# Two operands of a chunk made behind the next group's copies, the output product's sums and splits on VectorE, and block 0's reads reordered

## The chip, the cores and the metric

The kernel runs on one core of a Trainium2 chip. The core has five engines that run side by side and meet only at semaphores: TensorE (PE in the profile; its weight loads are PEld), VectorE (DVE), ScalarE (ACT), GpSimd (POOL) and SyncE (SP), which here issues nearly all DMAs. The metric is the device time of one execution in microseconds (us); lower is better. Times are the median of several runs; one further execution was profiled.

## The reference

Three stages on float32 data, one after the other:

```
# 1. attention in chunks of 32 queries, with 16 keys to the left, 8 to the right and 8 memory keys
a = exp(scale * q_c @ k_full.T - max);  out_c = (a / (sum(a) + 1e-9)) @ v_full
# 2. x: (3072, 512)
h = x @ w_in            # (3072, 2048)
x = (h * cos(h)) @ w_out  # (3072, 512)
# 3.
h = max(x @ w1, x @ w2, x @ w3)   # (3072, 768)
y = h @ w_out2                    # (3072, 512)
```

## The kernel before

All matmuls keep float32 accuracy by splitting each operand in a rounded part (hi, made by ACT as a copy to a shorter format) and the rest (lo, made by DVE or POOL as a subtraction of hi from the source); a product is then three passes, hi*hi, hi*lo and lo*hi (PASSES).

**Phase 1** (the first 620 us or so) does stages 1 and 2 in 6 blocks of 512 tokens, each of 16 slots. A slot f does `p1` (x @ w_in for 128 columns of h, 12 matmuls), `chain` (the h*cos(h) of it on ACT and DVE, and the preparing of weights), and `p2` of the slot two before (the product with w_out). Between them lies the attention of the next block, after a table of steps per slot: FIRST for block 0, SECOND and STEADY for the others. In such a table "T1" means: in this slot's chain DVE transposes the attention weights of double chunk 1 (line 286) and SP writes them to DRAM (`ptd`, two buffers, line 287); "l1" or "L1" reads them back in the other layout (`pt`, one buffer, line 292, three DMAs), a small l after the slot's matmuls in SP's order, a capital L at the slot's beginning; "V1" is the product with v (line 305), after which SP loads a later v (line 239). SP and PE take their instructions in the order in which the code is written.

**Phase 2** (from about 620 us) does stage 3 for three pairs of 1024 tokens. Both matmuls of it use a Winograd form of Strassen's scheme: 7 products (PRODUCTS) of half size in place of 8, for which sums and differences of operands are made beforehand and sums of products afterwards. For a pair, `quad(p, q)` does the 7 products of one weight matrix and one slice of d_ff: q = 3*fp + e, chunk fp = 0, 1, 2 and expert e = 0, 1, 2. One product is 6 matmuls. A quad has four PSUM banks, A, E, F and B; A, E and F take two products each: the first is copied out (`snap`: ACT copies a, p5 and p7, line 735) before the second is added on top of it (start=False). So the fifth product of a quad (T2, into bank A) can't start before the copy of a is done, the sixth (B22) not before p5, the seventh (T4) not before p7. The next quad takes the other four banks.

After a quad the results r11, r12, r21, r22 hold the maximum over the experts so far. After e = 2 they make the operands of the output product: `g_oper(n, c)`, n = 0 to 6 for chunk c: a copy on ACT (line 802) and a rest on DVE or POOL (line 803). Operands 0 and 1 are made inside the quad, 2 and 3 at its end (lines 778 and 779) with two differences on POOL (lines 780 and 781), 4 to 6 in the output product. At e = 2 of chunk 2 follows `pair_out(p)`: 7 products of 18 matmuls each (line 836), whose sums are made by ACT (line 821), DVE and POOL (line 824) and stored by SP. While it runs, the operands of the next pair's quads are made from x (`x_ops`; B11, T1, T3, B21, T2, B22, T4; lines 641 and 642), one per product, by ACT and by DVE or POOL.

ACT, DVE, POOL and SP do their instructions in program order; `keep` holds that order as the code is written, `live` counts the buffers of the weight pool (28), and `fetch` loads the weights of a quad three quads ahead.

Of the kernel before, what the change touches and what calls it, by code (L numbers as in the profile page):

```python
# [9 lines left out]
F32 = mybir.dt.float32  # L10
# [36 lines left out]

FIRST = {2: "S0", 3: "S1", 4: "S2", 5: "S3 E01", 6: "E23 N0", 7: "T0 N1", 8: "L0 T1 N2", 9: "V0 l1 T2", 10: "V1 l2 N3", 11: "T3", 12: "V2 l3", 14: "V3"}  # L50
SECOND = {0: "S0", 1: "S1", 2: "E01 S2", 3: "N0 S3", 4: "T0", 5: "E23 N1 L0 S4", 6: "V0 T1", 7: "L1 N2", 8: "S5 T2 N3", 9: "V1 E45", 10: "L2 S6 T3", 11: "V2", 12: "L3 S7", 13: "V3", 14: "E67"}
STEADY = {1: "N0", 2: "T0 N1", 3: "L0", 4: "S4", 5: "V0 T1 N2", 6: "L1", 7: "S5", 8: "V1 T2 N3", 9: "L2 E45", 10: "S6 T3", 11: "V2 l3", 12: "S7", 13: "V3", 14: "E67"}

# [12 lines left out]
NW, NTOP = 28, 2  # L66
# [11 lines left out]
def attn_moe_kernel(ctx, tc, qT, kT, vw, w_in, w_out, w3, w2o, out):  # L78
# [565 lines left out]
    def x_ops(p):  # L644

        u1, u2, v1, v2 = (x2["raw", b, k] for b in range(2) for k in range(2))

        def diff(o, a, b):
            keep(DVE.tensor_tensor(o, a, b, op=ALU.subtract))

        def b11():
            x_get("B11", u1, POOL)

        def t1():
            xs["t1"] = w_tile([128, 2, M], "xt", F32)
            diff(xs["t1"], v1, u1)
            x_get("T1", xs["t1"], DVE)
            live[0] -= 1

        def t3():  # L660
            diff(v1, v2, v1)

        def t2():
            xs["t2"] = w_tile([128, 2, M], "xt", F32)
            diff(xs["t2"], v2, xs["t1"])
            live[0] -= 1
            x_get("T2", xs["t2"], DVE)

        def b22():
            x_get("B22", v2, POOL)  # L670
            live[0] -= 1

        def t4():
            t = w_tile([128, 2, M], "xt", F32)
            diff(t, u2, xs["t2"])
            live[0] -= 1
            x_get("T4", t, DVE)
            live[0] -= 1

        def o3():  # L680
            x_get("T3", v1, POOL)
            live[0] -= 1

        def b21():
            x_get("B21", u2, DVE)
            live[0] -= 1

        def d1():
            xs["t1"] = w_tile([128, 2, M], "xt", F32)
            diff(xs["t1"], v1, u1)  # L690

        def d2():
            xs["t2"] = w_tile([128, 2, M], "xt", F32)
            diff(xs["t2"], v2, xs["t1"])

        def s1():
            x_get("T1", xs["t1"], DVE)
            live[0] -= 2

        def s2():  # L700
            x_get("T2", xs["t2"], DVE)
        return dict(d1=d1, d2=d2, s1=s1, s2=s2, b11=b11, t1=t1, t3=t3, o3=o3, b21=b21, t2=t2, b22=b22, t4=t4)

    def x_free():
        live[0] -= 6
# [14 lines left out]
    def quad(p, q):  # L720

        fp, e = divmod(q, 3)
        bk = dict(zip("AEFB", (t[:, :M] for t in banks(4))))
        seen = set()
        t = {}
        r = post.get(fp)

        def xo(name):
            t[name] = raw_tile(name) if e == 0 else tmp["pool"].tile([128, M], F32, tag="xo", name=name, bufs=6)
            return t[name]  # L730

        def snap(name, b, pool=None):
            o = tr.tile([128, M], F32, tag="r", name=name) if pool else xo(name)
            t[name] = o
            keep(ACT.activation(out=o, in_=bk[b], func=AF.Copy))  # L735

        def add(eng, o, a, b, op=ALU.add):
            keep(eng.tensor_tensor(o, a, b, op=op))  # L738

        for n, (b, i, half, name) in enumerate(PRODUCTS):  # L740
            product(bk[b], wq[p, q, i], half, x2[name], b not in seen, True)
            seen.add(b)
            if n == 0:
                snap("a", "A")
            elif n == 1:
                snap("p5", "E")
            elif n == 2:
                snap("p7", "F")
                add(POOL, t["p5"], t["p5"], t["p7"])
            elif n == 3:  # L750
                add(DVE, t["a"], t["a"], bk["B"])
                if e:
                    add(DVE, r["r11"], r["r11"], t["a"], ALU.max)
                    if e == 2:
                        g_oper(0, fp)
            elif n == 4:
                snap("u2", "A", True)
                add(POOL, t["p5"], t["p5"], t["u2"])
            elif n == 5:
                t["c12"] = raw_tile("c12") if e == 0 else tr.tile([128, M], F32, tag="r", name="c12")  # L760
                add(DVE, t["c12"], t["u2"], bk["E"])
                if e:
                    add(DVE, r["r12"], r["r12"], t["c12"], ALU.max)
                    add(DVE, r["r22"], r["r22"], t["p5"], ALU.max)
                    if e == 2:
                        g_oper(1, fp)
            else:
                add(DVE, t["p7"], t["u2"], bk["F"])
                if e:
                    add(DVE, r["r21"], r["r21"], t["p7"], ALU.max)  # L770
                else:
                    post[fp] = dict(r11=t["a"], r12=t["c12"], r21=t["p7"], r22=t["p5"])
            yield n
        for i in range(4):
            wq.pop((p, q, i))
            live[0] -= 1
        if e == 2:
            g_oper(2, fp)
            g_oper(3, fp)
            add(POOL, r["r11"], r["r22"], r["r11"], ALU.subtract)  # L780
            add(POOL, r["r21"], r["r21"], r["r11"], ALU.subtract)

    def raw_tile(name):
        return tmp["pool"].tile([128, M], F32, tag="raw", name=name, bufs=12)
# [3 lines left out]
    def g_oper(n, c):  # L788

        r = post[c]  # L790
        if n == 1:
            keep(DVE.tensor_tensor(r["r11"], r["r12"], r["r11"], op=ALU.subtract))
        elif n == 2:
            keep(POOL.tensor_tensor(r["r12"], r["r22"], r["r12"], op=ALU.subtract))
        if n in (0, 4):
            g = gp.tile([128, 2, M], F32R, tag="g", name="g")
        elif n in (1, 5):
            g = pre.tile([128, 2, M], F32R, tag="p", name="g")
        else:
            g = w_tile([128, 2, M], "g")  # L800
        src = r[G_SRC[n]]
        keep(ACT.activation(out=g[:, 0, :], in_=src, func=AF.Copy))  # L802
        keep((POOL if G_POOL[n] else DVE).tensor_tensor(g[:, 1, :], src, g[:, 0, :].bitcast(F32), op=ALU.subtract))  # L803
        hB[n, c] = g

    G_POOL = (1, 0, 1, 0, 1, 0, 0)

    def pair_out(p):

# [13 lines left out]
        def add(eng, o, a, b):  # L823
            keep(eng.tensor_tensor(o, a, b, op=ALU.add))  # L824
# [5 lines left out]
        for n, (b, _, _, _) in enumerate(PRODUCTS):  # L830
# [11 lines left out]
            for i in range(2):  # L842
                u = t[i]
                if n == 0:
                    snap(i, "a", "A")
                elif n == 1:
                    snap(i, "p5", "E")
                elif n == 2:
                    snap(i, "p7", "F")
                    add(POOL, u["p5"], u["p5"], u["p7"])  # L850
                elif n == 3:
                    add(DVE, u["a"], u["a"], bk[i]["B"])
                    put(i, 0, 0, u["a"])
                elif n == 4:
                    snap(i, "u2", "A", True)
                    add(POOL, u["p5"], u["p5"], u["u2"])
                    put(i, 1, 1, u["p5"])
                elif n == 5:
                    add(DVE, xo(i, "c12", True), u["u2"], bk[i]["E"])
                    put(i, 0, 1, u["c12"])  # L860
                elif not last:
                    add(DVE, u["p7"], u["u2"], bk[i]["F"])
                    put(i, 1, 0, u["p7"])
                else:
                    for h, eng in enumerate((SP, ACT)):
                        sl = slice(256 * h, 256 * h + 256)
                        add(DVE, u["p7"][:, sl], u["u2"][:, sl], bk[i]["F"][:, sl])
                        c0 = 2 * p * M + 256 * h
                        keep(eng.dma_start(out=out[256 + 128 * i:384 + 128 * i, c0:c0 + 256], in_=u["p7"][:, sl]))
# [183 lines left out]
    got = [AHEAD]  # L1053

    def fetch(upto):
        while got[0] <= upto and got[0] < NP * NG and live[0] + 4 <= NW:
            q_fetch(*divmod(got[0], NG))
            got[0] += 1

# [2 lines left out]
    for p in range(NP):  # L1062
        for q in range(NQ):
            for n in quad(p, q):
                if p == 0 and q == 0 and n < 3:
                    while len(rest) > (2, 1, 0)[n]:
                        p2(*rest.pop(0))
                if n == 0:
                    fetch(p * NG + q + AHEAD)
                if p + 1 < NP:  # L1070
# [3 lines left out]
                    elif (q, n) in DIFFS:  # L1074
                        ops[DIFFS[q, n]]()
        x_free()
        todo = [["b11"], ["s1"], ["o3"], ["b21"], ["s2"], ["b22"], ["t4"]] if p + 1 < NP else []
        for n in pair_out(p):
            if n in (1, 2, 3):
                for c in range(3):  # L1080
                    g_oper(3 + n, c)
# [61 lines left out]
```

## Time and profile before

| | |
|---|---|
| median of 3 runs | 995.16 us (992.09 to 995.8) |
| the profiled execution's own time | 993.47 us |
| its span, first to last instruction | 991.7 us |
| PE busy | 960.4 us (97%) |
| DVE, POOL, ACT busy | 619.5, 477.7, 460.6 us |
| mean granted clock of TensorE | 0.998 of full speed |

PE is busy nearly all the time. So what can be won or lost shows where PE idles, some 31 us of the span in all, and those stretches are found by the view of waits and the timeline of PE. A start in the timeline is when the instruction began on its engine; in brackets stands how long the engine sat idle before it and what released it.

### The profile page before, as it was taken

The page shows a single profiled execution, that of the slowest core. Times are in us where ns is not written, and L with a number is a line of the kernel's source. Part 1 is how long each engine was busy: PE and PEld are TensorE (multiplying, and loading weights), DVE is VectorE, ACT ScalarE, POOL GpSimd, SP SyncE. Part 2 cuts the span into 40 slices and gives each one's busy share as a digit, 9 for nine tenths or more (in the row PEclk, how much of TensorE's full clock was granted, in tenths as well). Part 3 has the DMA queues.
Part 4 walks back from the last instruction along what each step waited for, and adds up shares of the span by engine and source line. Part 5 has one row for each costly group of instructions (what it writes and reads, how often), then busy time and mean ns, then how long its engine had stood idle before and what let it go on. Part 6 is the DMA issues. An engine that isn't in the chain of part 4 may idle for free.

```text
span 991.7 us, 14609 instructions
## 1 busy us (share of the span) xinstructions
PE 960.4 (97%) x5373; PEld 770.2 (78%) x5373; DVE 619.5 (62%) x878; ACT 460.6 (46%) x802; POOL 477.7 (48%) x377
## 2 busy tenths in 40 slices
PE   8999999999999999999999999999999999999998
PEld 5666788888888888888888888877887778877786
DVE  7689656655567656765656565546585465845554
ACT  6567654545545554555445444433262332623223
POOL 3465435535344534443444444445492554925544
PEclk9999999999999999999999999999999999999999
DMA  9986633573557656754687368864639546394512
GB/s 269 333 305 199 192 127 109 165 201 143 188 199 235 222 194 203 221 186 170 200 249 249 121 221 301 296 211 131 236 135 389 170 149 232 142 389 149 188 36 86
DMA packets 75912, 201.76 MB, mean 203 GB/s; under 512 B 8256, under 2 KB 21056, under 8 KB 75840
## 3 DMA queue, kind: packets, MB, share of 16 engines
q1 hardware_dynamic: 75552, 200.56, 60.2%
q8 instruction: 43, 0.70, 0.3%
q10 hardware_dynamic: 288, 0.26, 0.1%
q14 instruction: 29, 0.24, 0.1%
HBM read 154.13 MB, written 46.66 MB: 202 GB/s over the span
## 4 chain that ended last, share of the span: by engine, by line
PE 74%; DVE 9%; DMA 7%; ACT 4%; POOL 3%; issue 2%; SPq 0%; DVEq 0%; POOLq 0%; ACTq 0%
PE h L392 23%; PE acc L392 22%; PE hb L712 21%; PE hb L836 3%; PE s L246 3%; DMA raw<-in_w_out_dram 2%; PE s L305 2%; DVE p L738 2%; DVE c L738 2%; POOL p L824 1%; DMA raw<-in_w_in_dram 1%; DMA k<-in_kT_dram 1%; ACT g L802 1%; DMA v<-in_vw_dram 1%; DVE g L803 1%
## 5 line engine op out<-in xcount | busy, mean ns | idle before, releaser
L392 PE MATMUL h<-x,w 128*128 128x512 f32 x1152 | 285.3, 397 | 0.0
L392 PEld LDWEIGHTS h<-x,w 128*128 128x128 f32 x1152 | 214.2, 189 | 49.1 <-issue 1.4
L462 POOL TENSOR_TENSOR g<-ki,g 128x512 fp32r<-128x512 f32 x80 | 108.3, 1354 | 213.0 <-ACT g L461 186.5
L712 PE MATMUL hb<-x,wq 128*128 128x512 f32 x648 | 156.9, 391 | 16.2 <-ACT a L735 16.2
L712 PEld LDWEIGHTS hb<-x,wq 128*128 128x128 f32 x648 | 121.0, 188 | 44.6 <-ACT a L735 19.6
L392 PE MATMUL acc<-g,w 128*128 128x512 f32 x576 | 138.3, 389 | 0.0
L392 PEld LDWEIGHTS acc<-g,w 128*128 128x128 f32 x576 | 108.1, 188 | 22.5
L712 PE MATMUL hb<-xo,wq 128*128 128x512 f32 x486 | 119.4, 390 | 1.5 <-DVE c L824 1.5
L392 PE MATMUL acc<-g,wa 128*128 128x512 f32 x480 | 115.6, 389 | 0.2 <-POOL g L462 0.2
L455 ACT ACTIVATE ki<-ki,pio 128x512 f32<-128x512 f32 x80 | 57.9, 724 | 109.4 <-DVE ki L453 109.3
L712 PEld LDWEIGHTS hb<-xo,wq 128*128 128x128 f32 x486 | 91.1, 188 | 21.2 <-DVE c L824 2.3
L392 PEld LDWEIGHTS acc<-g,wa 128*128 128x128 f32 x480 | 90.0, 188 | 19.3 <-POOL g L462 0.6
L452 DVE SCALAR_TENSOR_TENSOR ki<-h,ki 128x512 f32<-128x512 f32 x80 | 54.9, 687 | 68.8 <-ACT ki L450 68.8
L457 DVE TENSOR_TENSOR ki<-h,ki 128x512 f32<-128x512 f32 x80 | 55.2, 690 | 54.6 <-ACT ki L455 54.6
L738 POOL TENSOR_TENSOR p<-p,p 128x512 f32<-128x512 f32 x27 | 36.8, 1365 | 105.0 <-ACT p L735 105.0
L836 PE MATMUL hb<-g,wo 128*128 128x512 f32 x378 | 86.6, 390 | 0.0
L836 PEld LDWEIGHTS hb<-g,wo 128*128 128x128 f32 x378 | 70.8, 188 | 15.3 <-DVE g L803 0.6
L461 ACT ACTIVATE g<-ki 128x512 fp32r<-128x512 f32 x80 | 50.5, 632 | 59.3 <-DVE ki L457 59.1
L450 ACT ACTIVATE ki<-h 128x512 int32<-128x512 f32 x80 | 47.2, 589 | 59.7 <-PE h L392 53.3
L738 DVE TENSOR_TENSOR a<-a,hb 128x512 f32<-128x512 f32 x27 | 18.5, 684 | 69.0 <-PE hb L712 65.6
L553 DVE TENSOR_TENSOR wq<-raw,wq 128x512 fp32r<-128x512 f32 x36 | 44.1, 1244 | 24.4 <-ACT wq L552 24.4
L198 DVE SCALAR_TENSOR_TENSOR raw<-raw,top 128x512 int32<-128x512 int32 x48 | 47.3, 985 | 14.7 <-ACT top L181 14.5
(121 smaller groups left out, 1279.7 us busy)
## 6 DMA issues: line engine op xcount, KB each, us to landing
wq<-wd SPq DMA_DIRECT2D x81, 512.0 KB, 6.3
wa<-wad SPq DMA_DIRECT2D x40, 512.0 KB, 6.1
wo<-wod SPq DMA_DIRECT2D x30, 512.0 KB, 3.7
wd<-wq SPq DMA_DIRECT2D x27, 512.0 KB, 2.9
v<-in_vw_dram SPq DMA_DIRECT2D x24, 384.0 KB, 6.6
raw<-in_w_dram SPq DMA_DIRECT2D x18, 511.8 KB, 5.5
raw<-in_w_in_dram SPq DMA_DIRECT2D x16, 511.8 KB, 10.3
raw<-in_w_out_dram SPq DMA_DIRECT2D x16, 511.8 KB, 10.0
```

The costliest lines, as they stand in the source:

```text
L198: keep(DVE.scalar_tensor_tensor(o, z, 13, top[key], op0=ALU.logical_shift_right, op1=ALU.bitwise_or))
L392: PE.matmul(o, lhsT=w[a][:, sl], rhs=x[b], start=first and n == 0, stop=last and n == 2)
L450: row(ACT.activation(out=ki, in_=h, func=AF.Copy, scale=INV2PI, bias=0.25))
L452: row(DVE.scalar_tensor_tensor(c, h, INV2PI, ki, op0=ALU.mult, op1=ALU.subtract))
L455: row(ACT.activation(out=c, in_=c, func=AF.Sin, scale=2 * math.pi, bias=pio2))
L457: row(DVE.tensor_tensor(c, h, c, op=ALU.mult))
L461: row(ACT.activation(out=g[:, 0, :], in_=c, func=AF.Copy))
L462: row(POOL.tensor_tensor(g[:, 1, :], c, g[:, 0, :].bitcast(F32), op=ALU.subtract))
L553: keep(eng.tensor_tensor(w[:, 1, :], src, w[:, 0, :].bitcast(F32), op=ALU.subtract))
L712: keep(PE.matmul(o, lhsT=w[:, a, 256 * half + 128 * c:256 * half + 128 * c + 128], rhs=x[c][:, b, :], start=first and n == 0, stop=n == 5, ...
L738: keep(eng.tensor_tensor(o, a, b, op=op))
L836: keep(PE.matmul(bk[i][b], lhsT=w[:, s, x, 128 * i:128 * i + 128], rhs=g[:, y, :], start=b not in seen and c == 0 and m == 0, stop=c == 2 ...
```

## The change

It has three parts. First, in `quad` at e = 2, the two differences r12 = r22 - r12 and r11 = r22 - r11 are made at the end of the quad (on POOL, on DVE for chunk 2), but operands 2 and 3 and the last difference go into a list, `behind`, from which they are taken in the next quad after its third product, that is behind the copies a, p5 and p7; for chunk 2 they are taken in `pair_out` after its first product. Second, in `pair_out` the sums of p5, the rests of operands 4 to 6 (and of operands 0 and 2 for chunk 2), and in `x_ops` the rests of B11, T3, B22 and the others go to DVE, so POOL has nothing left to do there; T4's difference is made in place, in u2, two products earlier. Third, in FIRST the step T2 goes from slot 9 to slot 10, and l2 becomes L2 in slot 11.

```
--- before.py
+++ after.py
@@ -47,7 +47,7 @@
 
 
 
-FIRST = {2: "S0", 3: "S1", 4: "S2", 5: "S3 E01", 6: "E23 N0", 7: "T0 N1", 8: "L0 T1 N2", 9: "V0 l1 T2", 10: "V1 l2 N3", 11: "T3", 12: "V2 l3", 14: "V3"}
+FIRST = {2: "S0", 3: "S1", 4: "S2", 5: "S3 E01", 6: "E23 N0", 7: "T0 N1", 8: "L0 T1 N2", 9: "V0 l1", 10: "V1 T2 N3", 11: "L2 T3", 12: "V2 l3", 14: "V3"}
 SECOND = {0: "S0", 1: "S1", 2: "E01 S2", 3: "N0 S3", 4: "T0", 5: "E23 N1 L0 S4", 6: "V0 T1", 7: "L1 N2", 8: "S5 T2 N3", 9: "V1 E45", 10: "L2 S6 T3", 11: "V2", 12: "L3 S7", 13: "V3", 14: "E67"}
 STEADY = {1: "N0", 2: "T0 N1", 3: "L0", 4: "S4", 5: "V0 T1 N2", 6: "L1", 7: "S5", 8: "V1 T2 N3", 9: "L2 E45", 10: "S6 T3", 11: "V2 l3", 12: "S7", 13: "V3", 14: "E67"}
 
@@ -699,7 +699,29 @@
 
         def s2():
             x_get("T2", xs["t2"], DVE)
-        return dict(d1=d1, d2=d2, s1=s1, s2=s2, b11=b11, t1=t1, t3=t3, o3=o3, b21=b21, t2=t2, b22=b22, t4=t4)
+
+        def s3():
+            x_get("T3", v1, DVE)
+            live[0] -= 1
+
+        def s22():
+            x_get("B22", v2, DVE)
+            live[0] -= 1
+
+        def s11():
+            x_get("B11", u1, DVE)
+
+        def s21():
+            x_get("B21", u2, DVE)
+
+        def d4():
+            diff(u2, u2, xs["t2"])
+            live[0] -= 1
+
+        def s4():
+            x_get("T4", u2, DVE)
+            live[0] -= 1
+        return dict(d4=d4, s3=s3, s4=s4, s11=s11, s21=s21, s22=s22, d1=d1, d2=d2, s1=s1, s2=s2, b11=b11, t1=t1, t3=t3, o3=o3, b21=b21, t2=t2, b22=b22, t4=t4)
 
     def x_free():
         live[0] -= 6
@@ -775,10 +797,17 @@
             wq.pop((p, q, i))
             live[0] -= 1
         if e == 2:
-            g_oper(2, fp)
-            g_oper(3, fp)
-            add(POOL, r["r11"], r["r22"], r["r11"], ALU.subtract)
-            add(POOL, r["r21"], r["r21"], r["r11"], ALU.subtract)
+            eng = DVE if fp == 2 else POOL
+            add(eng, r["r12"], r["r22"], r["r12"], ALU.subtract)
+            add(eng, r["r11"], r["r22"], r["r11"], ALU.subtract)
+
+            def rest():
+                g_oper(2, fp)
+                g_oper(3, fp)
+                add(eng, r["r21"], r["r21"], r["r11"], ALU.subtract)
+            behind.append(rest)
+
+    behind = []
 
     def raw_tile(name):
         return tmp["pool"].tile([128, M], F32, tag="raw", name=name, bufs=12)
@@ -790,8 +819,6 @@
         r = post[c]
         if n == 1:
             keep(DVE.tensor_tensor(r["r11"], r["r12"], r["r11"], op=ALU.subtract))
-        elif n == 2:
-            keep(POOL.tensor_tensor(r["r12"], r["r22"], r["r12"], op=ALU.subtract))
         if n in (0, 4):
             g = gp.tile([128, 2, M], F32R, tag="g", name="g")
         elif n in (1, 5):
@@ -800,10 +827,8 @@
             g = w_tile([128, 2, M], "g")
         src = r[G_SRC[n]]
         keep(ACT.activation(out=g[:, 0, :], in_=src, func=AF.Copy))
-        keep((POOL if G_POOL[n] else DVE).tensor_tensor(g[:, 1, :], src, g[:, 0, :].bitcast(F32), op=ALU.subtract))
+        keep((POOL if n in (0, 2) and c < 2 else DVE).tensor_tensor(g[:, 1, :], src, g[:, 0, :].bitcast(F32), op=ALU.subtract))
         hB[n, c] = g
-
-    G_POOL = (1, 0, 1, 0, 1, 0, 0)
 
     def pair_out(p):
 
@@ -847,13 +872,13 @@
                     snap(i, "p5", "E")
                 elif n == 2:
                     snap(i, "p7", "F")
-                    add(POOL, u["p5"], u["p5"], u["p7"])
+                    add(DVE, u["p5"], u["p5"], u["p7"])
                 elif n == 3:
                     add(DVE, u["a"], u["a"], bk[i]["B"])
                     put(i, 0, 0, u["a"])
                 elif n == 4:
                     snap(i, "u2", "A", True)
-                    add(POOL, u["p5"], u["p5"], u["u2"])
+                    add(DVE, u["p5"], u["p5"], u["u2"])
                     put(i, 1, 1, u["p5"])
                 elif n == 5:
                     add(DVE, xo(i, "c12", True), u["u2"], bk[i]["E"])
@@ -1053,7 +1078,7 @@
     got = [AHEAD]
 
     def fetch(upto):
-        while got[0] <= upto and got[0] < NP * NG and live[0] + 4 <= NW:
+        while got[0] <= upto and got[0] < NP * NG and live[0] + 4 + 2 * len(behind) <= NW:
             q_fetch(*divmod(got[0], NG))
             got[0] += 1
 
@@ -1065,6 +1090,8 @@
                 if p == 0 and q == 0 and n < 3:
                     while len(rest) > (2, 1, 0)[n]:
                         p2(*rest.pop(0))
+                if n == 2 and behind:
+                    behind.pop()()
                 if n == 0:
                     fetch(p * NG + q + AHEAD)
                 if p + 1 < NP:
@@ -1074,8 +1101,10 @@
                     elif (q, n) in DIFFS:
                         ops[DIFFS[q, n]]()
         x_free()
-        todo = [["b11"], ["s1"], ["o3"], ["b21"], ["s2"], ["b22"], ["t4"]] if p + 1 < NP else []
+        todo = [["s11"], ["s1"], ["s3"], ["s21"], ["s2", "d4"], ["s22"], ["s4"]] if p + 1 < NP else []
         for n in pair_out(p):
+            if n == 0:
+                behind.pop()()
             if n in (1, 2, 3):
                 for c in range(3):
                     g_oper(3 + n, c)
```

On ACT, at the end of chunk 0 of pair 0 (u2, a, p5, p7 are copies from PSUM, g operands of the output product), before the change:

```order
L802 ACTIVATE g_5973<-a_5762 128x512
L735 ACTIVATE u2_5982<-hb_5928 128x512
L802 ACTIVATE g_5996<-a_5762 128x512
L802 ACTIVATE g_6008<-c12_5847 128x512
L802 ACTIVATE g_6011<-p7_5798 128x512
L735 ACTIVATE a_6026<-hb_6016 128x512
L735 ACTIVATE p5_6042<-hb_6017 128x512
L735 ACTIVATE p7_6050<-hb_6018 128x512
L735 ACTIVATE u2_6066<-hb_6016 128x512
```

and with it:

```order
L829 ACTIVATE g_5973<-a_5762 128x512
L757 ACTIVATE u2_5982<-hb_5928 128x512
L829 ACTIVATE g_5996<-a_5762 128x512
L757 ACTIVATE a_6019<-hb_6009 128x512
L757 ACTIVATE p5_6035<-hb_6010 128x512
L757 ACTIVATE p7_6043<-hb_6011 128x512
L829 ACTIVATE g_6046<-c12_5847 128x512
L829 ACTIVATE g_6049<-p7_5798 128x512
L757 ACTIVATE u2_6066<-hb_6009 128x512
```

The copies of operands 2 and 3 (from c12 and p7) have moved from in front of the next quad's a, p5 and p7 to behind them; the copy of operand 1 (g_5996) stays in front.

On DVE, at the end of the output product of pair 0 (x and xo2 operands of the next pair, p5, c12 and p7 sums of the output product, xt_6734 T4's difference), before the change:

```order
L642 TENSOR_TENSOR xo2_6639<-xs_6208,xo2_6639 128x512
L642 TENSOR_TENSOR xo2_6640<-xs_6208,xo2_6640 128x512
L642 TENSOR_TENSOR x_6671<-xt_6335,x_6671 128x512 x2
L824 TENSOR_TENSOR c12_6702<-u2_6663,hb_6479 128x512
L824 TENSOR_TENSOR c12_6705<-u2_6667,hb_6480 128x512
L824 TENSOR_TENSOR p7_6579<-u2_6663,hb_6481 128x512
L824 TENSOR_TENSOR p7_6582<-u2_6667,hb_6482 128x512
L649 TENSOR_TENSOR xt_6734<-xs_6208,xt_6335 128x1024
L642 TENSOR_TENSOR xo2_6736<-xt_6734,xo2_6736 128x512
L642 TENSOR_TENSOR xo2_6737<-xt_6734,xo2_6737 128x512
```

and with it (T4's difference is written to xs_6208):

```order
L642 TENSOR_TENSOR xo2_6639<-xs_6208,xo2_6639 128x512
L642 TENSOR_TENSOR xo2_6640<-xs_6208,xo2_6640 128x512
L849 TENSOR_TENSOR p5_6544<-p5_6544,u2_6663 128x512
L849 TENSOR_TENSOR p5_6546<-p5_6546,u2_6667 128x512
L642 TENSOR_TENSOR x_6671<-xt_6335,x_6671 128x512 x2
L649 TENSOR_TENSOR xs_6208<-xs_6208,xt_6335 128x1024
L849 TENSOR_TENSOR c12_6703<-u2_6663,hb_6472 128x512
L849 TENSOR_TENSOR c12_6706<-u2_6667,hb_6473 128x512
L642 TENSOR_TENSOR x_6671<-xs_6210,x_6671 128x512 x2
L849 TENSOR_TENSOR p7_6579<-u2_6663,hb_6474 128x512
L849 TENSOR_TENSOR p7_6582<-u2_6667,hb_6475 128x512
L642 TENSOR_TENSOR xo2_6735<-xs_6208,xo2_6735 128x512
```

The sums of p5 and the rests of B22 have come in from POOL, and T4's difference has moved in front of the sums c12 and p7, which wait for the last two products of the output. From operand 2 of chunk 2 to the end of T4, DVE now has 38 subtractions or sums of 128x512 and one of 128x1024; before it had 21 and one in that stretch, and POOL the others.

On SP, in slots 8 to 11 of block 0 (ptd is the DRAM copy of the attention weights, pt what is read back of it), before the change:

```order
L287 DMA ptd1_109<-sm_782 128x768
L169 DMA raw_1043<-in_w_in_dram 128x2047
L169 DMA raw_1045<-in_w_out_dram 128x2047
L548 DMA wad8_100<-w_1026 128x1024
L287 DMA ptd0_108<-sm_845 128x768
L239 DMA v_1115<-in_vw_dram 96x1024
L292 DMA pt_1117<-ptd1_109 32x4x256 x3
L548 DMA wad9_101<-w_1074 128x1024
L239 DMA v_1185<-in_vw_dram 96x1024
L292 DMA pt_1187<-ptd0_108 32x4x256 x3
```

and with it:

```order
L287 DMA ptd1_109<-sm_782 128x768
L169 DMA raw_1043<-in_w_in_dram 128x2047
L169 DMA raw_1045<-in_w_out_dram 128x2047
L548 DMA wad8_100<-w_1026 128x1024
L239 DMA v_1113<-in_vw_dram 96x1024
L292 DMA pt_1115<-ptd1_109 32x4x256 x3
L548 DMA wad9_101<-w_1074 128x1024
L287 DMA ptd0_108<-sm_845 128x768
L239 DMA v_1185<-in_vw_dram 96x1024
L292 DMA pt_1192<-ptd0_108 32x4x256 x3
```

The write of T2 (ptd0) has gone from in front of v and the reads of pt to behind them. It is SP's only move in the whole program, and PE's order doesn't change at all.

## Rows read from the trace of the kernel before

**Rows 1.** The page, part 1: busy time, share of the span, instructions.

```profile
PE 960.4 (97%) x5373; PEld 770.2 (78%) x5373; DVE 619.5 (62%) x878; ACT 460.6 (46%) x802; POOL 477.7 (48%) x377
```

**Rows 2.** PE's waits over the whole span: us in total, times, longest.

```profile
PE hb L712 <- ACT a L735: 16.2, 8, 2.2
...
PE s L305 <- DMA pt<-ptd: 3.4, 1, 3.4
```

**Rows 3.** Timeline of PE at the end of chunk 0, pair 0: start, us, instructions.

```profile
652.32 2.88 PE L712 MATMUL hb<-x,wq 128*128 128x512 f32 x12
655.04 2.88 PE L712 MATMUL hb<-xo,wq 128*128 128x512 f32 x12
660.11 3.01 PE L712 MATMUL hb<-x,wq 128*128 128x512 f32 x12 [2.19 <-ACT a L735]
```

**Rows 4.** Timeline of all engines in the same stretch.

```profile
655.00 0.63 ACT L802 ACTIVATE g<-a 128x512 fp32r<-128x512 f32 x1 [3.91 <-DVE a L792]
...
657.52 1.39 DVE L738 TENSOR_TENSOR p<-p,p 128x512 f32<-128x512 f32 x1
...
658.94 0.63 ACT L802 ACTIVATE g<-p 128x512 fp32r<-128x512 f32 x1 [1.94 <-DVE p L738]
659.48 0.58 ACT L735 ACTIVATE a<-hb 128x512 f32<-128x512 f32 x1
```

**Rows 5.** Timeline of PE behind the output product of pair 0.

```profile
743.20 2.88 PE L712 MATMUL hb<-x,wq 128*128 128x512 f32 x12
746.82 3.06 PE L712 MATMUL hb<-xo,wq 128*128 128x512 f32 x12 [0.74 <-DVE c L824]
751.41 3.06 PE L712 MATMUL hb<-x,wq 128*128 128x512 f32 x12 [1.54 <-ACT a L735]
```

**Rows 6.** Timeline of all engines in the same stretch.

```profile
748.49 1.21 DVE L649 TENSOR_TENSOR xt<-xs,xt 128x1024 f32<-128x1024 f32 x1
...
749.73 1.15 ACT L641 ACTIVATE xo<-xt 128x512 fp32r<-128x512 f32 x2 [12.03 <-DVE xt L649]
...
750.79 0.58 ACT L735 ACTIVATE a<-hb 128x512 f32<-128x512 f32 x1
```

**Rows 7.** Busy: PE, PEld, DVE, ACT, POOL; granted clock, DMA share, GB/s: output product.

```profile
714.40:743.20 28.80, 28.80 (x127) 23.57 (x126) 23.31 (x19) 16.81 (x32) 25.53 (x17) 1.00 0.47 171
```

**Rows 8.** Timeline: a sum on DVE alone, and one beside POOL.

```profile
642.42 0.69 DVE L738 TENSOR_TENSOR c<-c,c 128x512 f32<-128x512 f32 x1
...
651.92 1.29 POOL L738 TENSOR_TENSOR p<-p,u 128x512 f32<-128x512 f32 x1
651.96 1.80 DVE L738 TENSOR_TENSOR c<-c,c 128x512 f32<-128x512 f32 x1
```

**Rows 9.** Timeline of PE in block 0.

```profile
91.21 1.15 PE L305 MATMUL s<-pt,v 96*64 96x64 f32 x32
92.29 3.02 PE L392 MATMUL h<-x,w 128*128 128x512 f32 x12
95.15 2.88 PE L392 MATMUL acc<-g,w 128*128 128x512 f32 x12
101.42 1.22 PE L305 MATMUL s<-pt,v 96*64 96x64 f32 x32 [3.39 <-DMA pt<-ptd]
102.57 4.51 PE L392 MATMUL h<-x,w 128*128 128x512 f32 x12
```

**Rows 10.** As rows 7, behind the wait in block 0.

```profile
101.40:107.00 5.60, 5.58 (x45) 4.58 (x46) 0.69 (x1) 1.08 (x2) 1.86 (x2) 0.70 0.55 146
```

**Rows 11.** Timeline of SP in block 0.

```profile
93.81 0.33 SPq L287 DMA_DIRECT2D ptd<-sm  x1
...
94.67 1.47 SPq L292 DMA_DIRECT2D pt<-ptd  x3
```

**Rows 12.** Reads of pt issued from 94.7 to 95.7 us.

```profile
DMA to landing us min/median/max: 5.6/5.8/6.0
```

**Rows 13.** Reads of pt issued from 85.1 to 86.0 us.

```profile
DMA to landing us min/median/max: 3.7/3.8/3.9
```

## The prediction, as it was put on record before the changed kernel ran

> **What bounds the kernel now.** I read the page's busy times first: PE is busy 960.4 us of a span of 991.7 us [rows 1], so nothing but PE's idle time, 31.3 us, and what that idle time does to its clock can be won. The waits of PE come next: 16.2 us in 8 waits on ACT's copies into a (line 735), and one wait of 3.4 us for a read of pt in block 0 [rows 2]. Then PE's timeline around each of them.
>
> At the end of chunk 0 of pair 0 the groups of 12 matmuls start 2.72 us apart (652.32, 655.04), then the next starts at 660.11 in place of 657.76: 2.35 us lost, and its group takes 3.01 us and not 2.88, another 0.13 [rows 3]. What is late is the copy of a at 659.48, which the fifth product needs. It stands on ACT behind operand 3's copy at 658.94, and that waited for DVE's maximum of p7, 657.52 to 658.91 [rows 4]. The product that a is copied from had been done since 653.68, half a group behind 652.32. So it is ACT's order that holds PE up, not a lack of time. The same stall stands at six places (two chunk ends in each of three pairs).
>
> Behind the output product of pairs 0 and 1 there are two waits: 746.82 in place of 745.92 (0.90 us, for the sums c12, which hold a bank), and 751.41 in place of 749.54 (1.87 us, for a again, plus 0.18 in the slower group) [rows 5]. Here ACT's copy of a at 750.79 stood behind the copies of T4, which waited for T4's difference on DVE, 748.49 to 749.70 [rows 6].
>
> In block 0 V1 would follow the group at 95.15 by about 2.81 us, at 97.96, but starts at 101.42, 3.46 us later, and the group behind it takes 4.51 us where the one behind V0 took 3.02 [rows 9]: 1.49 us more, at a granted clock of 0.70 over 101.4 to 107.0 [rows 10], so part of it at the lower of the two levels, 1.2 GHz. After the chunk ends' gaps of 2.35 us no such slowing shows (3.01 us) [rows 3].
>
> **Part one: operands 2 and 3 behind the copies (chunk ends).** Nothing is added; ten instructions or so change places on ACT, POOL and DVE. ACT now does operand 1's copy (655.00 to 655.63 [rows 4]), then a at once, 0.58 us: done about 656.2. PE wants it at 657.76, 1.5 us later. p5 and p7 follow as their products end (655.04 and 656.40), the latter done at about 657.2, wanted by the seventh product at 660.48. The copies of operands 2 and 3 now wait on POOL's difference and DVE's maximum of 658.91 with only the copy u2 behind them on ACT. For u2 the cover is long: its bank is not written again before the quad after the next. DVE's own rest of operand 3 stays where it was, in front of the next sum, and the sums have the same room of a quad. POOL does the same six instructions in another order. I take the whole stall away: 6 x (2.35 + 0.15, between the 0.13 here and the 0.18 behind the output product [rows 5]) = 15.0 us. If the cover fails (ACT's a still late), the bound on the other side is 0, and a loss beyond that I see no reason for, since ACT does nothing earlier than it could have before.
>
> **Part two: the output product.** POOL did 25.53 us of work in pair 0's 28.8 us and DVE 23.31 [rows 7]. Now DVE has all of it: from operand 2 of chunk 2 to T4, 38 instructions of 128x512 and one of 128x1024. A sum on DVE with nothing on POOL takes 0.69 us; the same sum that began 0.04 us behind one of POOL took 1.80 [rows 8]. The Trainium skill, "SBUF — State Buffer", section "Who interferes with whom", says that a DVE instruction with two SBUF inputs and a GpSimd one that reads SBUF block each other for the whole instruction; the pair of rows agrees, since 1.80 is about POOL's 1.29 and the rest of 0.69.
>
> With POOL empty I take 0.69 us each, and 1.21 for the wide one [rows 6]. The list begins some 6 us into the product: at the mid chunk end DVE's maximum of p7 ends 6.6 us behind 652.32 [rows 3, 4], and here without POOL's interference in its last part. So it begins at about 720.4. The sums c12 are the 31st and 32nd of the narrow ones: 720.4 + 32 x 0.69 + 1.21 = 743.7. T3 of the next pair, which waits for their banks, comes at 743.0 + 2.72 = 745.7. T4's rests end 6 x 0.69 = 4.1 later, at 747.8, and T4 comes at 743.0 + 6 x 1.36 = 751.2. T4's copies on ACT, 1.15 us [rows 6], follow the difference, which ends two instructions before c12 does, at 742.3; so they are done at 743.5, and ACT is free for a when the first product ends at 744.4. Within the output product the fourth operand is wanted at 714.4 + 4 x 4.08 = 730.7, and stands 10th in the list, 727.3. So both waits go, 2 x (0.90 + 1.87 + 0.18) = 5.9 us. What is late next is c12, by a margin of 2.0 us. In the last pair there is no next pair, its end is PE's, and I count 0. Bounds: at 0.69 us DVE fits; at 1.80 us each [rows 8] c12 would come 34 us late. I take the near end, as the 1.80 needs a POOL at work.
>
> **Part three: block 0.** T2's write no longer stands on SP in front of V1's reads. SP took it at 93.81 and the reads from 94.67 [rows 11], 2.3 us behind V0's end at 92.36 [rows 9], though they need only that end and a write long done. Without it the reads start about 92.9, 1.8 us sooner. With the landing of before, 5.6 to 6.0 us [rows 12], the last would be there at 99.8; with that of the earlier reads, 3.7 to 3.9 [rows 13], at 97.8. V1 could run at 97.96. So the wait shrinks from 3.46 us to between 0 and 1.9, and the slow group's 1.49 goes, as gaps of 2.35 us cost no clock [rows 3]: 3.1 to 4.95 us, and I take 4.1. T2's write now comes a slot later, while V2 stays two slots behind; if all of V1's stall came back at V2, this part would be worth 0, and with an equally long stall at both it would cost 4.95 (my two ends of the range for it: -4.95 and 4.95).
>
> **The sum.** 15.0 + 5.9 + 4.1 = 25.0 us. The profiled execution took 993.47 us: 968.5. That execution lies 1.7 us below the median of the runs, 995.16, which would give 970.2; I say 969.
>
> **The rivals.**
> 1. The block 0 stall only moves to V2. For it: the new distance T2 to V2 is that of T1 to V1, which stalled. Against: T1's reads had a write in front of them, T2's don't, and V2's reads stand at their slot's beginning. Time: 968.5 + 4.1 = 972.6.
> 2. DVE is just too slow in the output product: at 0.85 us each, c12 comes at 720.4 + 32 x 0.85 + 1.21 = 748.8, 3.1 us late, twice 6.2, in place of the 5.9 won. Time: about 968.5 + 5.9 + 6.2 = 980.6. The margin is gone at (745.7 - 720.4 - 1.21) / 32 = 0.75 us. For it: waits between ACT and DVE in a list that is nearly full. Against: 0.69 and a POOL with nothing to do.
> 3. The chunk-end stall stays, as operand 1's copy still stands in front of a and itself waits for DVE (3.91 us idle [rows 4]). It would have to slip by 1.5 us. Time: 968.5 + 15.0 = 983.5.
> 4. Slower: DVE's rate doesn't fall when POOL's work comes over, so that the two loads add up: 23.31 + 25.53 = 48.8 us in 28.8 [rows 7], 20 us late, less the 3 us of room, at two pairs' ends: 34 us against 15.0 + 4.1 won. Time: 993.5 - 19.1 + 34 = 1008. It decides from a mean of about 1.1 us: two pair ends late by 10 us each. The Trainium skill, "Perfetto Trace Analysis", section "Optimizing Scalar/DVE Operations", warns that moving work between GpSimd and DVE might not help, as they share a read port. Against it: 0.69 beside 1.80 [rows 8].
>
> **How the numbers follow.** The forecast as summed 0.67, its own range 965 to 972; rival 1 0.13; rival 2 0.12; rival 3 0.05; rival 4 0.03. The range of 8 in 10, with the first rival whole, most of the second and the runs' own spread of 3 us: 965 to 978. A change under 0.5%, about 5 us, is what a measurement of this kernel can't tell from none. All cases but the fourth are faster by more than that; a mix of rivals 1, 2 and 3 could end within it: faster 0.94, same 0.03, slower 0.03.
>
> **What would show it.** Right: in the profile after, PE's waits on line 757 (the copy a) and on the c12 sums are gone or under 1 us in all; groups of 12 at chunk ends start 2.72 us apart; DVE's sums in the output product take 0.6 to 0.7 us; POOL is empty there; V1 waits under 2 us and no stretch of block 0 shows a clock of 0.70. Wrong: a PE wait on a rest of operands 4 to 6, on T3 or T4, or a new one at V2.

## The result and the profile after

The changed kernel takes 966.72 us (median of 5 runs, 966.13 to 968.57), against 995.32 us before on the same chip (992.09 to 995.9): a ratio of 0.9721, 95% interval 0.9702 to 0.9741. The forecast was 969 us, range 965 to 978. The profiled execution took 966.72 us against 993.47, its span is 964.6 us against 991.7. In the new kernel lines 712, 735, 738, 792, 802 and 824 of before are 734, 757, 760, 821, 829 and 849.

PE's waits over the whole span (as rows 2: us in total, times, longest):

```profile
PE warm L375 <- DVE zero L970: 1.5, 1, 1.5
PE s L356 <- issue: 1.2, 1, 1.2
PE warm L375 <- DVE x L365: 0.9, 1, 0.9
PE s L305 <- DMA pt<-ptd: 0.8, 1, 0.8
PE s L342 <- POOL sm L337: 0.5, 1, 0.5
PE s L356 <- DVE px L348: 0.3, 1, 0.3
PE s L356 <- ACT px L350: 0.2, 1, 0.2
PE acc L392 <- POOL g L462: 0.2, 1, 0.2
```

The first entry of [rows 2], 16.2 us on the copies of a, is gone, and V1's wait is 0.8 us in place of 3.4. All the others lie in the first 30 us or are 0.2 us long: in phase 2 PE waits for nothing. Its timeline at the end of chunk 0 (as rows 3), and behind the output product of pair 0 (as rows 5):

```profile
646.64 2.88 PE L734 MATMUL hb<-x,wq 128*128 128x512 f32 x12
649.36 2.88 PE L734 MATMUL hb<-xo,wq 128*128 128x512 f32 x12
652.08 2.88 PE L734 MATMUL hb<-x,wq 128*128 128x512 f32 x12
...
732.32 2.88 PE L734 MATMUL hb<-x,wq 128*128 128x512 f32 x12
735.04 2.88 PE L734 MATMUL hb<-xo,wq 128*128 128x512 f32 x12
737.76 2.88 PE L734 MATMUL hb<-x,wq 128*128 128x512 f32 x12
```

All groups start 2.72 us apart, where [rows 3] has 5.07 and [rows 5] 3.62 and 4.59. On the other engines at the chunk end (as rows 4):

```profile
649.31 0.63 ACT L829 ACTIVATE g<-a 128x512 fp32r<-128x512 f32 x1 [3.92 <-DVE a L821]
649.85 0.58 ACT L757 ACTIVATE a<-hb 128x512 f32<-128x512 f32 x1
...
651.84 1.28 DVE L760 TENSOR_TENSOR p<-p,p 128x512 f32<-128x512 f32 x1
...
653.16 0.63 ACT L829 ACTIVATE g<-p 128x512 fp32r<-128x512 f32 x1 [1.12 <-DVE p L760]
```

DVE's maximum of p7 comes hardly earlier in relation to the products than it did (6.48 us behind the group at 646.64, 6.59 before), and operand 3's copy still waits for it (1.12 us); but a is copied by 650.43, 1.65 us before the fifth product wants it at 652.08. On DVE at the end of the output product, and busy times in it (as rows 7):

```profile
727.11 1.22 DVE L649 TENSOR_TENSOR xs<-xs,xt 128x1024 f32<-128x1024 f32 x1
728.25 1.28 DVE L849 TENSOR_TENSOR c<-u,hb 128x512 f32<-128x512 f32 x2
...
733.12 1.29 DVE L642 TENSOR_TENSOR xo<-xs,xo 128x512 fp32r<-128x512 f32 x2
```

```profile
703.76:732.32 28.56, 28.56 (x128) 23.65 (x126) 26.38 (x42) 18.31 (x34) 0.19 (x1) 1.00 0.65 218
```

POOL fell from 25.53 us [rows 7] to 0.19, DVE rose only from 23.31 to 26.38. The mean of one instruction of DVE went from 1.23 us (19 in the window of [rows 7]) to 0.63 (42), so by an estimate from these means some 11 us, about half, of DVE's time there before was POOL's hold on it. Two sums in a row take 1.28 us, so 0.64 each. The sums c12 are done at 729.53, 5.5 us before T3 at 735.04, and T4's rests at 734.4, before T4 at 740.48.

In block 0 (as rows 9 and 11):

```profile
89.69 1.15 PE L305 MATMUL s<-pt,v 96*64 96x64 f32 x32
...
97.28 1.15 PE L305 MATMUL s<-pt,v 96*64 96x64 f32 x32 [0.77 <-DMA pt<-ptd]
98.37 3.02 PE L392 MATMUL h<-x,w 128*128 128x512 f32 x12
...
109.47 1.15 PE L305 MATMUL s<-pt,v 96*64 96x64 f32 x32
```

```profile
91.40 1.28 SPq L292 DMA_DIRECT2D pt<-ptd  x3
...
99.37 0.34 SPq L287 DMA_DIRECT2D ptd<-sm  x1
```

V1 follows V0 by 7.59 us, not 10.21, the group behind it takes 3.02 us and not 4.51, and V2 (109.47) waits for nothing.

Cut at the same instructions, the two profiled spans differ so: block 0 from V0 to V2 4.18 us (91.21 to 115.17 before, 89.69 to 109.47 after); the six chunk ends 14.9; the two waits behind the output products 5.9; the inside of two output products 0.22 each (28.78 and 28.56) and 0.14 at the end; and 1.52 ahead of V0, where no instruction was changed: the profiled execution of before happened to wait 1.4 us for a k read at 57 us, and this one did not. Together 27.1. That wait and V2, from the trace of before:

```profile
PE s L246 <- DMA k<-in_kT_dram: 1.4, 1, 1.4
```

```profile
115.17 1.15 PE L305 MATMUL s<-pt,v 96*64 96x64 f32 x32
```

### The profile page after: what moved, and what is told of

It reads as the page before. It is cut to its first block, busy times and chain, and to the rows that moved or that the text cites. A ratio compares the mean times of both kernels' runs of the same rounds, so it can differ in the third digit from the quotient of the medians.

```text
span 964.6 us, 14585 instructions
## 1 busy us (share of the span) xinstructions
PE 955.1 (99%) x5372; PEld 770.3 (80%) x5373; DVE 616.5 (64%) x926; ACT 461.4 (48%) x802; POOL 410.3 (43%) x329
## 4 chain that ended last, share of the span: by engine, by line
PE 94%; DVE 3%; ACT 1%; issue 1%; DMA 1%; POOL 0%; SPq 0%; DVEq 0%; ACTq 0%
PE hb L734 27%; PE h L392 26%; PE acc L392 23%; PE hb L861 9%; PE s L246 3%; PE acc L389 3%; PE s L305 2%; PE warm L375 1%; DMA pt<-ptd 1%; PE s L356 0%; ACT ki L455 0%; DVE ki L453 0%; DVE ki L452 0%; DVE ki L457 0%; DVE mx L322 0%
## 5 line engine op out<-in xcount | busy, mean ns | idle before, releaser
L198 DVE SCALAR_TENSOR_TENSOR raw<-raw,top 128x512 int32<-128x512 int32 x48 | 46.1, 960 | 13.1 <-ACT top L181 11.7
```

Of the source, the lines that this page charges most:

```text
L198: keep(DVE.scalar_tensor_tensor(o, z, 13, top[key], op0=ALU.logical_shift_right, op1=ALU.bitwise_or))
```

## The experiments

Ratios are against the kernel before on the same chip in the same rounds; "V0 to V1" is the distance of the two starts on PE. "Over the changed kernel" is between medians of different rounds; by the two ratios the 4.2, 26.6 and 6.5 us below come out as 4.7, 27.3 and 6.1.

**Each part alone.** First the new FIRST, nothing else:

```
-FIRST = {..., 9: "V0 l1 T2", 10: "V1 l2 N3", 11: "T3", ...}
+FIRST = {..., 9: "V0 l1", 10: "V1 T2 N3", 11: "L2 T3", ...}
```

> The kernel before with the new FIRST alone. Theory (the three parts are independent and add up): V1 in block 0 waits under 2 us instead of 3.4, the slow group behind it (4.51 us for 12 matmuls) goes back to about 3.0, 4.1 us less than before, so about 989 to 991 by the runs; all eight waits on the copies of a stay at about 16 us. Rival (the stall only moves to V2): no change in the time, a wait of 3 us before V2.

Ratio 0.9965 (0.9942 to 0.9988), 3.5 us. V1 waits 1.42 us, the group behind it takes 3.04, V2 waits for nothing, and the waits on a stay at 16.2 us. The rival falls. Then only the order of operands 2 and 3 of chunks 0 and 1, with the two differences at the quad's end and the condition in `fetch` that go with it:

```
+            def rest():
+                g_oper(2, fp)
+                g_oper(3, fp)
+                add(POOL, r["r21"], r["r21"], r["r11"], ALU.subtract)
+            if fp < 2:
+                behind.append(rest)
+            else:
+                rest()
...
+                if n == 2 and behind:
+                    behind.pop()()
```

> The kernel before with only the operands 2 and 3 of chunks 0 and 1 made behind the next quad's copies a, p5 and p7 (chunk 2 and the output product as before). Theory (ACT's order alone makes the chunk-end stall): six waits of 2.2 us gone, 15.0 us less than before; the waits behind the output product stay (0.74 and 1.55 us, twice). Rival (the stall is DVE's and POOL's load and only changes its place): under 7 us less, with PE waits on p5 or p7 copies in its place.

Ratio 0.9829 (0.9802 to 0.9856), 17.0 us, 14.3 to 19.7. PE's waits:

```profile
PE hb L712 <- ACT a L735: 3.1, 2, 1.6
PE s L305 <- DMA pt<-ptd: 2.3, 1, 2.3
PE hb L712 <- DVE c L831: 1.6, 2, 0.8
```

Six of the eight waits on a are gone, nothing stands in their place, and the two pair ends stay, as the theory has it. Third the output product alone, of whose edit two places are shown:

```
-                    add(POOL, u["p5"], u["p5"], u["p7"])
+                    add(DVE, u["p5"], u["p5"], u["p7"])
...
-        todo = [["b11"], ["s1"], ["o3"], ["b21"], ["s2"], ["b22"], ["t4"]]
+        todo = [["s11"], ["s1"], ["s3"], ["s21"], ["s2", "d4"], ["s22"], ["s4"]]
```

> The kernel before with only the output product's part of the change: its sums, rests and the next pair's operands on DVE, T4's difference in place and two products earlier; operands 2 and 3 of all chunks as before. Theory: the waits behind the output product go (0.74 and 1.55 us, twice), 5.9 to 6.3 us less than before, DVE 0.6 to 0.7 us an instruction; the six chunk-end waits stay. Rival (DVE becomes the bound there): POOL's share, 17 instructions per product, appears on DVE at over 1 us each, c12 later than before, no gain or a loss.

Ratio 0.9941 (0.9916 to 0.9967), 5.9 us, 3.3 to 8.4. Both pair ends are free of waits, six waits on a of 13.1 us in all remain, and DVE takes 0.68 to 0.69 us an instruction there. 3.5, 17.0 and 5.9 make 26.4; the whole change gave 27.8 by its ratio. The parts add up within their intervals.

**Why the output product fits on DVE.** The changed kernel with the moved work back on POOL:

```
-                    add(DVE, u["p5"], u["p5"], u["p7"])
+                    add(POOL, u["p5"], u["p5"], u["p7"])
...
-        keep((POOL if n in (0, 2) and c < 2 else DVE).tensor_tensor(g[:, 1, :], ...))
+        keep((POOL if n in (0, 2, 4) else DVE).tensor_tensor(g[:, 1, :], ...))
...
-            x_get("B11", u1, DVE)
+            x_get("B11", u1, POOL)
```

> The changed kernel with the output product's moved work back on POOL (sums of p5, rests of operands 0, 2 and 4 of the output product and of B11, T3 and B22, the two differences of chunk 2); T4's difference stays in place and early, all orders stay. Theory (it is taking the work off POOL that makes DVE's list fit): the list on DVE runs beside POOL at up to 1.8 us an instruction, T3 behind the output product waits about 2 us for c12 at two places, 4 to 5 us slower than the changed kernel. Rival (the earlier place of T4's difference does it all): within 1 us of the changed kernel, no PE wait behind the output product.

Median 970.95 us, ratio 0.9768 (0.9741 to 0.9795): 4.2 us over the changed kernel, and PE's only waits in phase 2 are for c12.

```profile
PE hb L734 <- DVE c L849: 4.1, 2, 2.2
```

So the early place of T4's difference frees the copy of a, but without taking the work off POOL it makes c12 later. Then useless work for POOL:

```
+            for _ in range(3):
+                s0, s1 = (t.bitcast(F32) for t in tops)
+                keep(POOL.tensor_tensor(s1, s0, s0, op=ALU.add))
             seen.add(b)
```

> The changed kernel with 21 useless sums of 128x512 on POOL in each output product (3 per product, on two tiles that nobody else uses by then; some 27 us of POOL work). Theory (DVE's and POOL's sums hold each other up): while POOL has work, DVE's sums with two SBUF inputs take 1.2 to 1.8 us instead of 0.69, c12 comes 10 to 20 us late, PE waits in and behind the output products, 25 to 60 us slower than the changed kernel. Rival (they don't, and 1.80 had another reason): 0.69 each and the same time.

Median 993.35 us, ratio 0.9995 (0.9974 to 1.0015): 26.6 us over the changed kernel. Groups on DVE in the first output product, and PE's longest wait:

```profile
L642 DVE TENSOR_TENSOR x<-xs,x 128x512 fp32r<-128x512 f32 x2 | 3.0, 1524 | 0.0
...
L642 DVE TENSOR_TENSOR xo<-xs,xo 128x512 fp32r<-128x512 f32 x4 | 2.6, 677 | 0.0
...
L760 DVE TENSOR_TENSOR p<-u,hb 128x512 f32<-128x512 f32 x1 | 0.7, 674 | 0.0
```

```profile
PE hb L861 <- DVE g L830: 15.7, 15, 4.2
```

The same kind of instruction takes 1.52 us while POOL has work and 0.68 after it has run out; the sum of the last line of the groups, which has one of its two inputs in PSUM (hb), took 0.67 us in the midst of POOL's work. This is what the Trainium skill's "SBUF — State Buffer", section "Who interferes with whom", says of DVE instructions with two SBUF inputs, and it decides here against the warning of the Trainium skill's "Perfetto Trace Analysis", section "Optimizing Scalar/DVE Operations": the work is worth moving because POOL is left with none. PE's 15 waits all lie inside the output products, for rests of their operands. The sums c12 came 41.3 us behind the first product's start instead of 25.8, as late as forecast, but PE was as late itself, and the waits behind the output products, which the theory had too, did not come.

**Which copy has to be in front.** The list is taken two products sooner:

```
-                if n == 2 and behind:
+                if n == 0 and behind:
```

> The changed kernel with the list behind taken two products sooner, behind the copy of a but ahead of p5 and p7. Theory (what counts is which copy from PSUM stands behind operand 3's copy on ACT): the sixth product waits for p5 in place of the fifth for a, 0.9 to 1.1 us at each of the six chunk ends, 6 to 7 us slower than the changed kernel. Rival (any place behind a will do): the same time. Second rival (the whole 2.35 us back): 15 us slower.

Median 973.25 us, ratio 0.9782 (0.9758 to 0.9806): 6.5 us over the changed kernel, with six waits on p5 (4.7 us in all by the view of waits, 0.7 to 1.1 each; 6.6 when the six chunk ends of the two profiles are compared by starts, which takes in the slower groups behind) and none on a. The first theory holds to the place and the size.

**What held V1's reads.** The kernel before, with T2's write issued by ACT:

```
-        keep(SP.dma_start(out=ptd[d % 2], in_=m))
+        keep((ACT if d == 6 else SP).dma_start(out=ptd[d % 2], in_=m))
```

> The kernel before with one DMA moved: the write of T2's transposed weights in block 0's slot 9 is issued by ACT instead of SP, at the same time; the reads for V1 no longer stand behind it on SP. Theory (the position on SP delays the reads): the reads start at about 92.9 us of the span instead of 94.7, V1 waits under 2 us and the slow group behind it goes, 3 to 4 us less than before. Rival (the 384 KB of the write, in the DMA engines ahead of the reads, delays them): the reads start 1.8 us sooner but land at the same time, V1 still waits 3 us, no gain.

Ratio 0.9976 (0.9951 to 1.0001), 2.4 us: clear neither of no change nor of the theory's 3 to 4 us. The reads start 1.63 us behind V0's start, not 3.46, but take 5.7 to 6.4 us to land (4.9 to 5.0 in the changed kernel); V1 waits 2.27 us, V0 to V1 is 9.09 us, and the group behind takes 4.61. In the six profiles with the new order, whose reads start as early, V0 to V1 is 7.25 to 8.24 us; in the six with the old order and SP's write 9.14 to 10.26. That looks as if the write in flight beside the reads cost V1 0.85 us or more, but the landings don't bear it out. Here are those of this run, of the new FIRST alone (no write near) and of the run with only the operands moved (the write on SP 0.9 us ahead):

```profile
DMA to landing us min/median/max: 5.7/5.8/6.4
...
DMA to landing us min/median/max: 5.6/5.7/5.9
...
DMA to landing us min/median/max: 4.5/4.7/4.7
```

The reads landed in 4.6 to 5.9 us in the six profiles with the new order and in 4.5 to 6.0 in the six with the write on SP. So one profile of ACT's write, whose slowest read took 0.4 us longer than any of the others, doesn't show that the write delays them. The profile lies between the theory (V1's wait under 2 us, no slow group) and the rival (still 3 us), and neither is settled by this run. The other way round, the changed kernel with the reads ahead of v's load:

```
                 a_v(d)
+                if d == 4:
+                    a_l(5)
                 a_load_v(d + 2)
```

> The changed kernel with the reads for V1 in slot 9 issued ahead of the load of v instead of behind it. Theory (the reads start when V0 has freed their buffer, and queue behind 384 KB of v): they start 0.5 us sooner and land over 0.8 us sooner, V1's last wait of 0.77 us goes, and 0.8 us less in the profile, which the runs can hardly tell. Rival (they land no sooner, since the transfers share the DMA engines anyway): the wait stays at 0.5 to 0.8 us.

Median 966.73 us, ratio 0.9716 (0.9691 to 0.974). The reads land in 3.6 to 3.8 us, V1 waits no more (V0 to V1 6.75 us). This last 0.8 us can't be told from the changed kernel by time.

**Slow groups.** In the profile of the new FIRST alone two chunk ends had groups of 4.31 and 4.61 us, where the forecast had counted on no such thing. So the kernel before was profiled twice more, unchanged:

> The kernel before, unchanged, profiled a second time. New theory (each idle stretch of 2.2 to 3.4 us of PE lowers its clock in some executions and not in others, and then costs 1.3 to 1.6 us more in the group behind it): some of the six chunk ends, 0 to 3, show a group of 12 matmuls of 4.2 to 4.6 us where the first profile showed none, and the span rises by 1.5 us for each. Rival (the chunk ends always cost 2.5 us, the slow groups came from the edits in block 0 or in the output product): none, as in the first profile.

> The kernel before, unchanged, profiled a third time; expected as for the second. Between the profiles of one kernel the number of slow groups differs if the theory holds, and the same number at the same places speaks for a cause in the program's order.

They took 995.19 and 996.09 us (one run each). The first has two slow groups at the chunk ends, of pairs 0 and 1, the second has two, both in pair 2. From the second, an end without a slow group and one with it, and their busy rows in the columns of [rows 7]:

```profile
781.78 3.02 PE L712 MATMUL hb<-x,wq 128*128 128x512 f32 x12 [2.17 <-ACT a L735]
...
904.18 4.61 PE L712 MATMUL hb<-x,wq 128*128 128x512 f32 x12 [2.17 <-ACT a L735]
```

```profile
904.20:908.60 4.40, 4.40 (x12) 3.54 (x13) 1.05 (x2) 1.50 (x3) 3.22 (x3) 0.61 0.35 85
781.80:784.60 2.80, 2.80 (x12) 2.34 (x13) 1.05 (x2) 1.51 (x3) 2.20 (x2) 1.00 0.32 121
```

The waits are the same to 0.01 us; the granted clock (third number from the end) over the group behind is 0.61 in the one case, so mostly the lower level of 1.2 GHz, and 1.00 in the other. The place differs between executions of one kernel, so it is not in the program's order. Then the gaps were made longer in the kernel before (one useless copy on ACT, `if fp < 2`, behind operand 3), and a short one was made in the changed kernel (the list taken at n == 0, with the same copy behind it):

```
+                s0, s1 = (t.bitcast(F32) for t in tops)
+                keep(ACT.activation(out=s1, in_=s0, func=AF.Copy))
```

> The kernel before with one useless copy on ACT (128x512, about 0.6 us) ahead of the next quad's copy of a at the six chunk ends, which makes the gaps of 2.35 us about 2.9. Theory (the clock falls the oftener the longer the gap): more slow groups of 4.2 to 4.6 us than in the kernel before, 3 to 6 of the six, so 3.3 us for the gaps and up to 1.5 us more for each slow group, 5 to 10 us slower than before. Rival (the falls don't depend on the gap's length): 3.3 us slower, and 0 to 3 slow groups.

> The changed kernel with the list behind taken behind the copy of a (as in the run y3_zero) and one useless copy on ACT behind it at the six chunk ends: the sixth product waits for p5 by about 1.3 to 1.5 us instead of 0.7. Theory: no slow group at all, 9 to 10 us slower than the changed kernel (3.5 slower than y3_zero), and a spread of the runs as narrow as the changed kernel's. Rival (a gap of any length lowers the clock now and then): some groups of over 2 us for 6 matmuls, and 11 us or more.

The longer gaps: ratio 1.006 (1.0037 to 1.0082), 6 us slower, waits of 2.69 to 2.71 us and four slow groups of six. The short ones: waits of 1.23 to 1.65 us and no slow group in the profile, whose six chunk ends took 3.1 us more than with the list at n == 0 alone; median 976.48 us, ratio 0.9833 (0.9779 to 0.9886), which is 9.8 us over the changed kernel by the medians and 11.1 by the ratios, where the theory had 9 to 10 and the rival 11 or more. One forecast of the theory failed: the spread isn't narrow. One of its four runs took 982.19 us at a mean granted clock of 0.997, the other three 976.17 to 976.73 at 1.00. That run was not profiled, so a slow group behind a short gap isn't excluded.

Over the profiles, a wait at a chunk end of 1.65 us or less was followed by a slow group 0 times of 12, one of 2.16 to 2.19 us 11 times of 36 (six kernels and executions that keep that stall), one of 2.7 us 4 times of 6. The same traces hold other waits of PE, behind the output products, for V1, and in the run with useless work for POOL: of 1.53 to 1.84 us none of 15 was followed by a stretch at the lower clock, of 2.23 to 2.33 us one of 4, of 2.87 to 4.21 us all 6. So the longer gap was followed by it oftener; why some gaps of the same length are and others not stays open.

## Why the prediction was right, and where its sizes were off

**Chunk ends: right, and probably some 2 us too small.** The profiles show what was summed, 14.9 us of gaps against 15.0. The part alone gave 17.0 (14.3 to 19.7), which doesn't exclude 15.0 by itself. The step that failed is "gaps of 2.35 us cost no clock", read from one execution in which none of the six did [rows 3]. In 11 of 36 cases such a gap was followed by a group some 1.4 us slower, so over six of them 2.6 us an execution that the sum left out. The spread of five runs each, 966.13 to 968.57 after and 992.09 to 995.9 before, fits that but is too few to show it.

**Output product: right.** 5.9 us forecast, 5.9 in the two profiles and in the part alone. Off were two terms of DVE's list: it began 4.6 us behind the product's start and not 6.0, and 0.69 us was one instruction by itself, where in a row they start 0.60 to 0.65 us apart. So c12 came 25.8 us behind the product's start instead of 29.3 (1.4 us by the start, 2.1 by the pace) and had 5.5 us to spare instead of 2.0. So rival 2 was further off than priced. Rival 4's mechanism is real (1.52 beside 0.68 us) but needs POOL at work. Rivals 2 and 4 are excluded here by the profile after, not only improbable. The 0.22 us inside each output product were counted as nothing.

**Block 0: right, in size and for the most part in its reason.** 4.1 forecast; 4.18 in the profiles, 3.5 (1.2 to 5.8) in the runs of that part. The forecast's first term was the start of the reads, 1.8 us earlier. In the six profiles with the old order they start 3.44 to 3.46 us behind V0's start, in the six with the new 1.71 us: 1.74 earlier. V0 to V1 is 2.2 us shorter in the mean of each six, so the start is most of it and some 0.5 us is left for a quicker landing, in ranges that overlap (4.5 to 6.0 us and 4.6 to 5.9). In the one run with ACT issuing the write the reads started as early and V1 gained little, and why is not settled. What the forecast had wrong was to read two terms from one execution: the before of [rows 9] had one of the longest landings and a slow group behind V1, which came in four of the six profiles with the old order and in none with the new. V0 to V2 is 21.3 to 24.6 us in those six and 19.4 to 20.5 with the new order; the means differ by 3.5 us, as in the runs of the part. Rival 1 falls: V2 has no wait in any profile with the new order.

**The sum.** 25.0 us forecast, 26.75 between the two profiled executions, of which 1.5 lies ahead of V0 and isn't the change's; 28.6 between the medians. By the ratio it is 27.8 (25.8 to 29.7), a little more than forecast beyond the noise. The clock's 2.6 us at the chunk ends, less 0.6 in block 0, would bring 25.0 to 27.0; that is worked out from counts and means, not measured by itself. The opening's reads, which put V0 between 88.68 and 91.21 us in the profiles whatever the kernel, blur it by as much.

Rival 3 was near enough to name its margin: a is copied 1.65 us before it is wanted (1.5 forecast), and operand 1's copy still waits 3.92 us for DVE ahead of it.

## What to carry to other kernels

When the busiest engine waits a little at regular places, look for what stands in front of the released instruction on its releaser: here a copy whose input had been ready for 5.8 us stood in line behind one that was still waiting, and a change of order with no work saved was worth 1.7%. Before work is moved between GpSimd and VectorE, measure the target's instruction with the source idle; the times beside each other say what they cost each other, not what the work costs. Price a stall of PE from several executions: the clock behind it may differ from one to the next.

## What the runs showed of the hardware

TensorE's clock behind a gap is not settled by the gap alone: 2.32 us before V1 in the run with only the operands moved was followed by a group of 3.01 us, 2.27 us with T2's write on ACT by one of 4.61 at a granted clock of 0.61. Sums on DVE of 128x512 in float32 take 0.69 us alone and 0.64 in a row, and 1.52 to 1.80 beside GpSimd's sums when both inputs lie in SBUF; with one input in PSUM a sum took 0.67 beside them. Three 128 KB reads landed in 3.6 to 3.8 us ahead of a 384 KB load (one profile), in 4.6 to 5.9 behind it (six), in 4.5 to 6.0 behind it and a 384 KB write (six), and in 5.7 to 6.4 with such a write issued beside them by ACT (one).
